# Attention: phi from transposed queries, its norms from narrow matmuls

## The chip, the cores and the metric
The program runs on one core of a Trainium2 chip. A core has five engines that run side by side and wait for each other on semaphores: PE (TensorE, matmuls and transposes), DVE (VectorE), ACT (ScalarE), POOL (GpSimd) and SP, which only issues DMAs here. The metric is the device time of one execution in microseconds (us).

## The reference
The program is one attention with a linear memory, then two mixture-of-experts layers. The change touches only the attention:

```
B, H, S, D = 4, 8, 576, 64
scores = (1/sqrt(D)) q k^T, causal;  a = softmax(scores);  local = a v
phi(x) = where(x > 0, x, exp(x) - 1) + 1          # = min(exp(x), 1) + max(x, 0)
q_p = phi(q)
mem_ret  = q_p M_prev            # (S x 64) (64 x 64) per batch and head
mem_norm = q_p . z_prev + 1e-6   # one number per row
g = sigmoid(beta)                # one number per head
out = g * mem_ret / mem_norm + (1 - g) * local
```

## The kernel before
The attention works through 16 units; unit u is one batch and one pair of heads. Each unit has 576 rows: four blocks of 128 and a tail of 64. The loop over u is software-pipelined in five slots n = 0 to 4: in slot n it issues the scores of a row block of unit u (`score`, blocks 3, 2, 1, 0 and the tail, which is block 4), a part of the second half of unit u-1, and a part of the transposes of unit u+1. A scheduler then places the instructions of each engine in one fixed order, in which they wait for semaphores; so the order is not quite that of the code.

The second half of a unit transposes the softmax numerators P (`ptrans`), and `av` accumulates both terms of the output in one PSUM tile x: first the memory term, `Mb` (M_prev of both heads on the diagonal) against `pT` (phi transposed), then P^T against v. The two heads of a pair each use 64 columns of the PE array, and their matmuls stand next to each other (L306). The result is multiplied with R (1 over the softmax sums, spread over 64 rows for each head, L307) into xT. So the memory term must hold g / mem_norm times the softmax sum before.

phi is made from the queries as they lie in memory (rows on the partitions, `phi_a`): exp on ACT (L126), max on POOL (L127), min and add on DVE (L128), times z on POOL (L131); DVE sums over d and inverts (`phi_b`, L149 to L153); POOL multiplies phi with the factor (L155, L167, `phi_c`). Then PE transposes the scaled phi (`trans` part 2) and ACT copies it to pT (L209). The sums' inverses go a way of their own: POOL spreads them to `rr` (L164), PE transposes them (L173, `inverse`), ACT copies them to R (L174). The tail's P is multiplied with its inverse sum on POOL (L255, `norm`).

PSUM tiles of the tag "t" (all transposes, x) have four buffers, so each waits for the copy out of the tile four before it. After units 3, 7, 11 and 15 the router of the first expert layer works on a batch of rows. The expert layers start when the attention and the router's table are done.

Of the kernel before, what the change touches and what calls it, by code (L numbers as in the profile page):

```python
# [19 lines left out]
NP = H // 2  # L20
# [7 lines left out]
def attention(ctx, tc, q, k, v, M_prev, z_prev, beta, xT, ident, router=None):  # L28
# [50 lines left out]
    Mb = []  # L79
    for i in range(2):  # L80
        t = c1.tile([128, NP, 128], F32, name=f"Mb{i}")
        nc.gpsimd.memset(t, 0.0)
        Mb.append(t)

    zt, ld, ph, un = {}, {}, {}, {}

    nrm, Rs = [], []
    for i in range(2):
        t = c1.tile([128, NT, 2], F32, name=f"nrm{i}")
        nc.vector.memset(t, 1.0)  # L90
        nrm.append(t)
        t = c1.tile([128, S], F32, name=f"R{i}")
        nc.gpsimd.memset(t[:, 512:], 1.0)
        Rs.append(t)

    def load_b(b):
        zt[b] = nat.tile([128, DM], F32, tag="z", name="zb", bufs=2)
        nc.sync.dma_start(zt[b], z_prev[b].rearrange("h d -> (h d)")[None, :].to_broadcast([128, DM]))
        for h in range(2):
            src = M_prev[b].rearrange("(a two) d e -> two d a e", two=2)[h]  # L100
            nc.sync.dma_start(Mb[b % 2][h * 64:(h + 1) * 64, :, h * 64:(h + 1) * 64], src)

    def load(u, names):

# [13 lines left out]

    def phi_a(u):

        b, a = divmod(u, NP)
        ex = tmp.tile([128, NT, 128], F32, tag="ex", name="ex")
        qp = tmp.tile([128, NT, 128], F32, tag="qp", name="qp")
        z = zt[b][:, a * 128:(a + 1) * 128]
        for e, p, qn in zip(parts(ex), parts(qp), parts(ld[u, "q"])):
            nc.scalar.activation(e, qn, AF.Exp)  # L126
            (nc.gpsimd if u else nc.vector).tensor_scalar(p, qn, 0.0, None, ALU.max)  # L127
            nc.vector.scalar_tensor_tensor(p, e, 1.0, p, ALU.min, ALU.add)  # L128
        zb = z[:, None, :].to_broadcast([128, 4, 128]), z[:64]
        for e, p, zz in zip(parts(ex), parts(qp), zb):  # L130
            nc.gpsimd.tensor_tensor(e, p, zz, ALU.mult)  # L131
        ph[u] = ex, qp
# [11 lines left out]
    def phi_b(u):  # L144

        a = u % NP
        ex, qp = ph[u]
        n = nrm[u % 2]
        nc.vector.tensor_reduce(n[:, :4], ex[:, :4].rearrange("p i (h d) -> p i h d", h=2), AX.X, ALU.add)  # L149
        nc.vector.tensor_reduce(n[:64, 4], ex[:64, 4].rearrange("p (h d) -> p h d", h=2), AX.X, ALU.add)  # L150
        nc.vector.tensor_scalar(n, n, 1e-6, None, ALU.add)
        nc.vector.reciprocal(n, n)
        nc.vector.tensor_tensor(n, n, gt[:, None, 2 * a:2 * a + 2].to_broadcast([128, NT, 2]), ALU.mult)  # L153
        pv = qp[:64, 4].rearrange("p (h d) -> p h d", h=2)
        nc.gpsimd.tensor_tensor(pv, pv, n[:64, 4, :, None].to_broadcast([64, 2, D]), ALU.mult)  # L155

    def phi_c(u):

        su, n = un[u]["su"], nrm[u % 2]
        nc.vector.tensor_scalar(su[:, :4], su[:, :4], 1e-9, None, ALU.add)  # L160
        rc = sm.tile([128, 4, 2], F32, tag="rc", name="rc", bufs=2)
        nc.vector.reciprocal(rc, su[:, :4])
        rr = un[u]["rr"] = tmp.tile([128, 4, 128], F32, tag="rr", name="rr")
        nc.gpsimd.tensor_copy(rr.rearrange("p i (h d) -> p i h d", h=2), rc[:, :, :, None].to_broadcast([128, 4, 2, D]))  # L164
        nc.vector.tensor_tensor(n[:, :4], n[:, :4], su[:, :4], ALU.mult)
        pv = ph[u][1][:, :4].rearrange("p i (h d) -> p i h d", h=2)
        nc.gpsimd.tensor_tensor(pv, pv, n[:, :4, :, None].to_broadcast([128, 4, 2, D]), ALU.mult)  # L167
# [8 lines left out]
    def phi_t(u):  # L176
        if "pT" not in un[u]:
            un[u]["pT"] = tr.tile([128, S], F32, tag="pT", name="pT")
        return un[u]["pT"]

    def trans(u, part):


        qt = qTp[u % 2]
        p = ps_t.tile([128, 512], F32, tag="t", name="tp")
        if part == 0:
            un[u] = {"kT": tr.tile([128, S], F32, tag="kT", name="kT"), "P": {}}
        if part < 3:
            src = (ld.get((u, "k")), ld.get((u, "q")), ph[u][1] if u in ph else None)[part]
            for i in range(4):  # L190
                nc.tensor.transpose(p[:, i * 128:(i + 1) * 128], src[:, i], ident)
        else:
            src = []
            if part == 3:
                src += [ld[u, "k"], ld[u, "q"]]
                if u > 0:
                    src.append(ph[u - 1][1])
            else:
                src += [ph[u][1]]
            for n, t in enumerate(src):  # L200
                nc.tensor.transpose(p[:, n * 64:(n + 1) * 64], t[:64, 4], ident[:64, :64])

        if part == 0:
            nc.vector.tensor_copy(un[u]["kT"][:, :512], p)
        elif part == 1:
            nc.scalar.activation(qt[:, 256:512], p[:, 256:], AF.Copy, scale=0.125)
            nc.vector.tensor_scalar(qt[:, :256], p[:, :256], 0.125, None, ALU.mult)
        elif part == 2:
            nc.scalar.copy(phi_t(u)[:, :512], p)  # L209
        elif part == 3:  # L210
# [3 lines left out]
            if u > 0:  # L214
                nc.vector.tensor_copy(phi_t(u - 1)[:, 512:], p[:, 128:192])
        else:
            nc.vector.tensor_copy(phi_t(u)[:, 512:], p[:, 0:64])

    def score(u, i):

# [3 lines left out]
        s = ps_s.tile([128, 2, 512], F32, tag="s", name="s")  # L224
        nm = sm.tile([128, 2], F32, tag="nm", name="nm")
        if i == 3:
            un[u]["su"] = sm.tile([128, NT, 2], F32, tag="su", name="su", bufs=2)
        sums = un[u]["su"][:, i]
        if i < 4:
            w = (i + 1) * 128  # L230
            for h in range(2):
# [18 lines left out]
    def norm(u):  # L250

        P, r = un[u]["P"][4], un[u]["su"][:, 4, 0:1]
        nc.vector.tensor_scalar(r, r, 1e-9, None, ALU.add)
        nc.vector.reciprocal(r, r)
        nc.gpsimd.tensor_scalar(P, P, r, None, ALU.mult)  # L255
# [64 lines left out]
    for u in range(NU + 1):  # L320
# [9 lines left out]
        for n in range(5):  # L330
            if sc:
                score(u, (3, 2, 1, 0, 4)[n])
                if n == 4:
                    phi_c(u)
            if ex:
                if n == 0:
                    norm(u - 1)
                    ptrans(u - 1, 5)
                    ptrans(u - 1, 4)
                elif n < 3:  # L340
                    ptrans(u - 1, 2 * n - 2)
                    ptrans(u - 1, 2 * n - 1)
                    if n == 1:
                        inverse(u - 1)
                    else:
# [942 lines left out]
```

## Time and profile before
| | before |
|---|---|
| median of 3 runs (lowest to highest) | 2078.16 us (2076.13 to 2081.61) |
| the profiled execution: its time, its span | 2078.23 us, 2076.5 us |
| busy share of the span: PE, DVE, ACT, POOL | 98%, 71%, 41%, 37% |
| scores of unit 3 start, scores of unit 15 start | 57.01 us, 252.83 us |
| last matmul of the attention ends about | 275.2 us |

The span is the time from the first to the last instruction that the profiler saw; the device time of that execution is 1.7 us longer. The attention is the first eighth of the span. A matmul in f32 shows as two records (two pieces, each with its own weight load, PEld); "x4" in a row is four such records one after the other. Ends of matmuls are modelled, so rates are read from starts.

### The profile page before, as it was taken

The page shows a single profiled execution, that of the slowest core. Times are in us where ns is not written, and L with a number is a line of the kernel's source. Part 1 is how long each engine was busy: PE and PEld are TensorE (multiplying, and loading weights), DVE is VectorE, ACT ScalarE, POOL GpSimd, SP SyncE. Part 2 cuts the span into 40 slices and gives each one's busy share as a digit, 9 for nine tenths or more (in the row PEclk, how much of TensorE's full clock was granted, in tenths as well). Part 3 has the DMA queues.
Part 4 walks back from the last instruction along what each step waited for, and adds up shares of the span by engine and source line. Part 5 has one row for each costly group of instructions (what it writes and reads, how often), then busy time and mean ns, then how long its engine had stood idle before and what let it go on. Part 6 is the DMA issues. An engine that isn't in the chain of part 4 may idle for free.

```text
span 2076.5 us, 31532 instructions
## 1 busy us (share of the span) xinstructions
PE 2038.2 (98%) x11528; PEld 1768.1 (85%) x11528; DVE 1480.6 (71%) x2573; ACT 853.7 (41%) x1808; POOL 776.9 (37%) x800
## 2 busy tenths in 40 slices
PE   7999999999899999999999999999999999999998
PEld 4666669999698998998888999899888899899987
DVE  6788757666786776667786677777678676677775
ACT  4656536555634333333343333333334433333332
POOL 6666511000133344344454334334355333333332
PEclk9999999999999999999999999999999999999999
DMA  7332146665611233444432222222223222122221
GB/s 189 83 75 78 33 153 229 202 210 170 215 51 61 68 67 69 62 66 77 61 107 67 61 77 66 62 76 67 62 62 111 62 63 80 61 64 79 62 62 40
DMA packets 238520, 187.35 MB, mean 90 GB/s; under 512 B 71440, under 2 KB 194320, under 8 KB 238352
## 3 DMA queue, kind: packets, MB, share of 16 engines
q1 hardware_dynamic: 229008, 171.48, 30.2%
q0 software_dynamic: 3520, 9.46, 1.3%
q10 hardware_dynamic: 5824, 4.25, 0.7%
q8 instruction: 95, 1.56, 0.3%
q14 instruction: 73, 0.60, 0.1%
HBM read 171.51 MB, written 13.64 MB: 89 GB/s over the span
## 4 chain that ended last, share of the span: by engine, by line
PE 46%; issue 16%; POOL 8%; DVE 3%; ACT 1%; POOLq 0%; DVEq 0%; ACTq 0%
PE y L1092 24%; PE prod L1021 21%; POOL T L913 4%; POOL w1l L907 3%; DVE w2l L907 0%; DVE c L1035 0%; DVE u L1035 0%; POOL out_dram L394 0%; DVE hl L1044 0%; PE lq L1133 0%; DVE S2l L907 0%; ACT hh L1039 0%; DVE A11l L907 0%; DVE A12l L907 0%; DVE csum L1166 0%
## 5 line engine op out<-in xcount | busy, mean ns | idle before, releaser
L1039 ACT ACTIVATE hh<-c 128x384 fp32r<-128x384 f32 x384 | 202.0, 526 | 837.3 <-DVE c L1035 837.2
L907 POOL TENSOR_TENSOR w1l<-T,w1h 128x1024 fp32r<-128x1024 f32 x94 | 226.7, 2412 | 851.0 <-ACT w1h L907 851.0
L1092 PE MATMUL y<-w2h,hh 128*128 128x512 f32 x1152 | 453.8, 394 | 0.0
L1092 PE MATMUL y<-w2l,hh 128*128 128x512 f32 x1152 | 453.8, 394 | 0.0
L1092 PE MATMUL y<-w2h,hl 128*128 128x512 f32 x1152 | 453.0, 393 | 0.0
L1044 DVE SCALAR_TENSOR_TENSOR hl<-c,hh 128x384 fp32r<-128x384 f32 x384 | 415.4, 1099 | 1.4 <-ACT hh L1039 1.0
L1035 DVE TENSOR_TENSOR c<-prod,u 128x384 f32<-128x384 f32 x288 | 160.3, 557 | 157.2 <-PE prod L1021 156.7
L1092 PEld LDWEIGHTS y<-w2h,hh 128*128 128x128 f32 x1152 | 216.5, 188 | 32.7
L1092 PEld LDWEIGHTS y<-w2h,hl 128*128 128x128 f32 x1152 | 216.5, 188 | 28.3
L1092 PEld LDWEIGHTS y<-w2l,hh 128*128 128x128 f32 x1152 | 216.7, 188 | 27.8
L913 POOL TENSOR_TENSOR T<-r,T 128x256 f32<-128x256 f32 x188 | 157.8, 840 | 14.1 <-issue 7.0
L913 POOL TENSOR_TENSOR T<-r 128x256 f32<-128x256 f32 x188 | 158.8, 845 | 7.1
L1035 DVE TENSOR_TENSOR u<-prod,u 128x384 f32<-128x384 f32 x192 | 106.0, 552 | 58.3 <-PE prod L1021 58.0
L1035 DVE TENSOR_TENSOR u<-prod,p 128x384 f32<-128x384 f32 x96 | 53.5, 557 | 127.2 <-PE prod L1021 127.1
L907 DVE TENSOR_TENSOR w2l<-r,w2h 128x512 fp32r<-128x512 f32 x188 | 137.1, 729 | 0.5 <-ACT w2h L907 0.5
L907 ACT CAST w2h<-r 128x512 fp32r<-128x512 f32 x188 | 106.7, 610 | 0.0
L907 DVE TENSOR_TENSOR w1l<-r,w1h 128x512 fp32r<-128x512 f32 (+1 forms) x188 | 104.6, 557 | 0.0
L1035 DVE TENSOR_TENSOR c<-prod,p 128x384 f32<-128x384 f32 x96 | 53.4, 557 | 68.8 <-PE prod L1021 64.1
L907 ACT CAST w1h<-T 128x1024 fp32r<-128x1024 f32 x94 | 97.0, 1032 | 1.0 <-POOL T L913 1.0
L1049 ACT COPY p<-prod 128x384 f32<-128x384 f32 x96 | 46.1, 480 | 120.8 <-PE prod L1021 120.6
L1103 DVE SCALAR_TENSOR_TENSOR acc<-y,P,acc 128x512 f32<-128x512 f32 x126 | 92.5, 744 | 4.3 <-PE y L1092 4.3
L907 ACT CAST w1h<-r 128x512 fp32r<-128x512 f32 (+1 forms) x188 | 94.5, 503 | 0.0
(386 smaller groups left out, 4202.9 us busy)
## 6 DMA issues: line engine op xcount, KB each, us to landing
r<-in_moe_w_dram SPq DMA_DIRECT2D x188, 512.0 KB, 4.5
r<-in_moe_w_dram SPq DMA_DIRECT2D x188, 256.0 KB, 2.9
xr<-xs_sorted SPq DMA_DIRECT2D x22, 256.0 KB, 5.1
kn<-in_k_dram SPq DMA_DIRECT2D x32, 128.0 KB, 2.6
qn<-in_q_dram SPq DMA_DIRECT2D x32, 128.0 KB, 2.7
vn<-in_v_dram SPq DMA_DIRECT2D x32, 128.0 KB, 2.8
xs_sorted<-zrow ACTq DMA_DIRECT2D x16, 256.0 KB, 3.1
zb<-in_z_prev_dram SPq DMA_DIRECT2D x4, 256.0 KB, 3.8
```

What stands on the lines that cost most here:

```text
L907: return (lambda: nc.scalar.copy(hi, src)), (lambda: eng.tensor_tensor(lo, src, hi.bitcast(F32), ALU.subtract))
L913: sub = lambda i, a, b: (lambda: nc.gpsimd.tensor_tensor(T[:, i], a, b, ALU.subtract))
L1021: nc.tensor.matmul(p, a[:, kd], b[:, kd], start=(i == 0), stop=(i == 5))
L1035: nc.vector.tensor_tensor(st[o], a, st[b], ALU.add)
L1039: nc.scalar.activation(hh[:, f, a * HT:(a + 1) * HT], st[o], AF.Relu)
L1044: nc.vector.scalar_tensor_tensor(hl[:, f, w], st[o], 0.0, hh[:, f, w].bitcast(F32), ALU.max, ALU.subtract)
L1049: nc.scalar.copy(st["p1"], p)
L1092: nc.tensor.matmul(yt[t], a[:, f, t * 128:(t + 1) * 128], b[:, f], start=(j == 0 and f == 0 and i == 0), stop=(j == NJ - 1 and f == 1 and ...
L1103: nc.vector.scalar_tensor_tensor(acc[t], yt[t], P[:, m, e:e + 1], acc[t], ALU.mult, ALU.add)
```

## The change
phi is now made from the transposed queries, which the scores need anyway (`qTp`, scaled by 1/8, so exp and relu take scale 8): exp and relu on ACT, min and add on DVE, straight into pT. The norms come from five matmuls for each unit whose stationary operand is a 128-column block of pT and whose moving operand is `Zb`, 128 x 2: z of one head in each column (tile `nb`). `sums` inverts norms and softmax sums together, multiplies the first four blocks' norm inverses with the sums, spreads all to `rr` (now 9 x 128 wide) and scales the tail's P. `inverse` transposes two sets of four blocks instead of one: the first multiplies pT in place on DVE, the second goes to R. The tail's block of `rr` is transposed in `ptrans` k = 7. g is multiplied into Mb when it is loaded; z is loaded as a column instead of spread over 128 partitions.

```diff
     def load_b(b):
-        zt[b] = nat.tile([128, DM], F32, tag="z", name="zb", bufs=2)
-        nc.sync.dma_start(zt[b], z_prev[b].rearrange("h d -> (h d)")[None, :].to_broadcast([128, DM]))
+        z = nat.tile([128, NP], F32, tag="z", name="zc", bufs=2)
+        zv = z_prev[b].rearrange("(a two) d -> two d a", two=2)
         for h in range(2):
+            r = slice(h * 64, (h + 1) * 64)
+            nc.sync.dma_start(z[r], zv[h])
...
+            nc.gpsimd.tensor_tensor(Mb[b % 2][r, :, r], Mb[b % 2][r, :, r],
+                                    gtm[r, :, None].to_broadcast([64, NP, D]), ALU.mult)
+            nc.gpsimd.tensor_copy(Zb[b % 2][r, :, h], z[r])
     def phi_a(u):
...
+        nc.scalar.activation(ex[:, :512], qt[:, :512], AF.Exp, scale=8.0)
+        nc.scalar.activation(rl[:, :512], qt[:, :512], AF.Relu, scale=8.0)
+        p = un[u]["pT"] = tr.tile([128, S], F32, tag="pT", name="pT")
+        nc.vector.scalar_tensor_tensor(p, ex, 1.0, rl, ALU.min, ALU.add)
+    def phi_b(u):
...
+        x = ps_t.tile([128, NT, 2], F32, tag="t", name="nb")
+        for i in range(NT):
+            o = min(i * 128, S - 128)
+            nc.tensor.matmul(x[:, i], un[u]["pT"][:, o:o + 128], Zb[b % 2][:, a], start=True, stop=True)
+        nc.vector.tensor_scalar(un[u]["nw"][:, :NT], x, 1e-6, None, ALU.add)
+    def sums(u):
...
+        nc.vector.tensor_scalar(nw[:, n:w], nw[:, n:w], 1e-9, None, ALU.add)
+        nc.vector.reciprocal(iv[:, :w], nw[:, :w])
+        nc.vector.tensor_tensor(iv[:, :8], iv[:, :8], nw[:, n:n + 8], ALU.mult)
+        rr = un[u]["rr"] = tmp.tile([128, 9, 128], F32, tag="rr", name="rr")
+        nc.gpsimd.tensor_copy(rr.rearrange("p i (h d) -> p (i h) d", h=2), iv[:, :18, None].to_broadcast([128, 18, D]))
+        P = un[u]["P"][4]
+        nc.gpsimd.tensor_scalar(P, P, iv[:, w - 1:w], None, ALU.mult)
     def inverse(u):
-        p = ps_t.tile([128, 512], F32, tag="t", name="rp_")
-        for i in range(4):
-            nc.tensor.transpose(p[:, i * 128:(i + 1) * 128], un[u]["rr"][:, i], ident)
-        nc.scalar.copy(Rs[u % 2][:, :512], p)
+        pT = un[u]["pT"]
+        for n in range(2):
+            p = ps_t.tile([128, 512], F32, tag="t", name="rp_")
+            for i in range(4):
+                nc.tensor.transpose(p[:, i * 128:(i + 1) * 128], un[u]["rr"][:, 5 * n + i], ident)
+            if n == 0:
+                nc.vector.tensor_tensor(pT[:, :512], pT[:, :512], p, ALU.mult)
+            else:
+                nc.scalar.copy(Rs[u % 2][:, :512], p)
     def ptrans(u, k):
...
+            nc.tensor.transpose(p[:, 128:256], un[u]["rr"][:, 4], ident)
+            pT = un[u]["pT"]
+            nc.vector.tensor_tensor(pT[:, 512:], pT[:, 512:], p[:, 192:256], ALU.mult)
...
             if ex:
                 if n == 0:
-                    norm(u - 1)
+                    sums(u - 1)
...
                     if n == 1:
                         inverse(u - 1)
-                    else:
-                        trans(u - 1, 2)
```

On PE, early in a steady unit, between the transposes of P blocks 2 and 3 and the next scores, before the change (tp is the PSUM tile of a transpose, kn the keys):

```order
L276 MATMUL tp_1440<-ident,P_1273 128x128
L276 MATMUL tp_1440<-ident,P_1235 128x128
L276 MATMUL tp_1440<-ident,P_1273 128x128
L276 MATMUL tp_1440<-ident,P_1235 128x128
L191 MATMUL tp<-ident,kn 128x128 x4
L233 MATMUL s<-kT,qTp_134 128x384 x2
```

and after:

```order
L258 MATMUL tp_1607<-ident,P_1450 128x128
L258 MATMUL tp_1607<-ident,P_1407 128x128
L258 MATMUL tp_1607<-ident,P_1450 128x128
L258 MATMUL tp_1607<-ident,P_1407 128x128
L142 MATMUL nb<-Zb_147,pT 128x2 x5
L190 MATMUL tp<-ident,kn 128x128 x4
L222 MATMUL s<-kT,qTp_139 128x384 x2
```

The five norm matmuls stand in front of the key transposes, and all later work of PE in the unit stands behind them.

On PE, later in the unit, from the transposes of the tail's P to the tail's scores, before the change:

```order
L283 MATMUL tp_1532<-ident,P_1381 128x128 x4
L289 MATMUL tp_1539<-ident,P_1381 64x128
L298 MATMUL x<-pT,Mb_140 128x256
L306 MATMUL x<-pt,vn 64x256 x2
L306 MATMUL x<-pt,vn 64x128 x2
L201 MATMUL tp<-ident,kn 128x64
L201 MATMUL tp<-ident,qn 128x64
L201 MATMUL tp<-ident,qp 128x64
L243 MATMUL s<-kT,qTp_134 128x288 x2
```

and after:

```order
L265 MATMUL tp_1517<-ident,P_1363 128x128 x4
L271 MATMUL tp_1524<-ident,P_1363 64x128
L283 MATMUL x<-pT,Mb_145 128x256
L291 MATMUL x<-pt,vn 64x256
L273 MATMUL tp_1524<-ident,rr 128x128
L291 MATMUL x<-pt,vn 64x256
L291 MATMUL x<-pt,vn 64x128 x2
L193 MATMUL tp<-ident,kn 128x64
L193 MATMUL tp<-ident,qn 128x64
L232 MATMUL s<-kT,qTp_139 128x288 x2
```

The tail's transpose of `rr` (L273) now stands between the matmuls of the two heads (the pair 64x256). It stands so in 13 of the 16 units; in the other three it splits the pair 64x128.

On POOL, one steady unit, from one scaling of the tail's P to the next, before:

```order
L255 TENSOR_SCALAR P_927<-P_927,su 128x576
L141 TENSOR_TENSOR vn<-vn,om 128x512
L142 TENSOR_TENSOR vn<-vn,om 64x128
L127 TENSOR_SCALAR qp<-qn 128x512
L127 TENSOR_SCALAR qp<-qn 64x128
L131 TENSOR_TENSOR ex<-qp,zb 128x512
L131 TENSOR_TENSOR ex<-qp,zb 64x128
L164 COPY rr<-rc 128x512
L167 TENSOR_TENSOR qp<-qp,nrm_142 128x512
L155 TENSOR_TENSOR qp<-qp,nrm_146 64x128
L255 TENSOR_SCALAR P_1115<-P_1115,su 128x576
```

and after:

```order
L152 TENSOR_TENSOR vn<-vn,om 128x512
L153 TENSOR_TENSOR vn<-vn,om 64x128
L167 TENSOR_SCALAR P_1738<-P_1738,iv 128x576
L165 COPY rr<-iv 128x1152
L152 TENSOR_TENSOR vn<-vn,om 128x512
L153 TENSOR_TENSOR vn<-vn,om 64x128
L167 TENSOR_SCALAR P_1921<-P_1921,iv 128x576
```

Five of POOL's instructions are gone, and the spread of the inverses, which stood ahead of the scaling of the tail's P, now stands behind it.

## Rows read from the trace of the kernel before

**Rows 1.** Windows: stretch, us, busy us of PE, PEld, DVE, ACT, POOL; clock, DMA, GB/s.
```profile
25.00:30.00 5.00, 2.89 (x12) 1.81 (x13) 4.74 (x16) 2.99 (x8) 2.90 (x4) 0.68 0.89 219
57.01:252.83 195.82, 192.14 (x1380) 120.97 (x1377) 154.14 (x409) 116.30 (x350) 117.84 (x133) 1.00 0.27 69
106.94:121.91 14.97, 14.53 (x110) 9.24 (x106) 12.69 (x32) 9.81 (x31) 9.58 (x12) 1.00 0.24 54
121.91:136.26 14.35, 14.33 (x109) 9.26 (x105) 11.89 (x30) 9.00 (x29) 8.69 (x11) 1.00 0.36 83
```

**Rows 2.** Waits of PE's weight loads, 57.01 to 252.83: us, times, longest.
```profile
PEld x L298 <- ACT pT L209: 3.8, 12, 0.4
...
PEld tp L191 <- issue: 1.6, 3, 0.6
...
PEld x L298 <- DVE pt L290: 1.5, 3, 0.6
```

**Rows 3.** Timeline of the expert stage at the f32 matmul with 8 columns.
```profile
588.73 0.28 PE L1025 MATMUL prod<-csum,one 128*128 128x8 f32 x2
588.84 0.19 PEld L1092 LDWEIGHTS y<-w2l,hh 128*128 128x128 f32 x1
588.86 0.48 PE L1092 MATMUL y<-w2l,hh 128*128 128x512 f32 x1
588.95 0.19 PEld L1092 LDWEIGHTS y<-w2h,hl 128*128 128x128 f32 x1
```

**Rows 4.** Timeline of PE in the unit that starts at 121.91.
```profile
126.13 0.60 PE L173 MATMUL rp__1669<-ident,rr 128*128 128x128 f32 x4
126.57 0.60 PE L191 MATMUL tp<-ident,qn 128*128 128x128 f32 x4
...
130.04 0.27 PE L289 MATMUL tp<-ident,P 128*64 128x128 f32 x1
130.34 0.70 PE L298 MATMUL x<-pT,Mb 128*128 128x256 f32 x2
130.97 0.87 PE L306 MATMUL x<-pt,vn 128*64 128x256 f32 x8
131.77 0.27 PE L201 MATMUL tp<-ident,kn 64*128 64x64 f32 x1
...
133.19 0.78 PE L298 MATMUL x<-pT,Mb 128*128 128x320 f32 x2
```

**Rows 5.** Timeline of PE: a head pair split by router transposes, and one whole.
```profile
88.29 1.12 PE L233 MATMUL s<-kT,qTp 64*128 64x512 f32 x2
89.34 0.66 PE L507 MATMUL lp<-ident,lt 128*128 128x128 f32 x4
...
106.94 1.13 PE L233 MATMUL s<-kT,qTp 64*128 64x512 f32 x4
108.00 0.29 PE L235 MATMUL s<-mk,idb 128*128 128x128 bf16 x2
```

**Rows 6.** Groups by line, 57.01 to 252.83: busy us, mean ns, idle before.
```profile
L255 POOL TENSOR_SCALAR P<-P,su 128x576 f32<-128x576 f32 x12 | 20.7, 1723 | 1.0 <-DVE nrm L150 1.0
...
L128 DVE SCALAR_TENSOR_TENSOR qp<-ex,qp 128x512 f32<-128x512 f32 (+1 forms) x24 | 17.7, 736 | 18.1 <-POOL qp L127 18.1
...
L164 POOL COPY rr<-rc 128x512 f32<-128x512 f32 x12 | 7.3, 609 | 23.1 <-DVE nrm L165 23.1
```

**Rows 7.** Timeline of the last unit: tail scores, their exp, P's scaling, inverses.
```profile
263.61 0.19 PE L244 MATMUL s<-mk,idb 128*128 128x64 bf16 x1
...
265.26 0.19 ACT L247 ACTIVATION_READ_ACCUMULATOR P<-s,nm 128x1 f32 x1
...
266.02 1.73 POOL L255 TENSOR_SCALAR P<-P,su 128x576 f32<-128x576 f32 x1 [2.34 <-DVE su L254]
...
268.29 0.38 PE L173 MATMUL rp__3447<-ident,rr 128*128 128x128 f32 x2
```

**Rows 8.** Timeline of PE in the second unit, at the second block of scores.
```profile
27.11 1.65 PE L233 MATMUL s<-kT,qTp 64*128 64x384 f32 x4 [2.80 <-ACT P L247]
```

More of the change, by code (lines that the diff above doesn't have):

```diff
@@ L71, in attention @@
     nc.vector.tensor_scalar(om, gt, -1.0, 1.0, ALU.mult, ALU.add)
+    gtm = c1.tile([128, NP], F32, name="gtm")
+    gtv = gt.rearrange("p (a two) -> p a two", two=2)
+    nc.vector.tensor_copy(gtm[0:64], gtv[0:64, :, 0])
+    nc.vector.tensor_copy(gtm[64:128], gtv[64:128, :, 1])
     qTp = []
@@ L78, in attention @@
         qTp.append(t)
-    Mb = []
+    Mb, Zb = [], []
     for i in range(2):
[L81 to L87, printed above, removed]
+        for to, nm, w in ((Mb, "Mb", 128), (Zb, "Zb", 2)):
+            t = c1.tile([128, NP, w], F32, name=f"{nm}{i}")
+            nc.gpsimd.memset(t, 0.0)
+            to.append(t)
+    ld, ph, un = {}, {}, {}
+    Rs = []
     for i in range(2):
-        t = c1.tile([128, NT, 2], F32, name=f"nrm{i}")
-        nc.vector.memset(t, 1.0)
-        nrm.append(t)
         t = c1.tile([128, S], F32, name=f"R{i}")
@@ L96, in load_b @@
     def load_b(b):
-        zt[b] = nat.tile([128, DM], F32, tag="z", name="zb", bufs=2)
-        nc.sync.dma_start(zt[b], z_prev[b].rearrange("h d -> (h d)")[None, :].to_broadcast([128, DM]))
+        z = nat.tile([128, NP], F32, tag="z", name="zc", bufs=2)
+        zv = z_prev[b].rearrange("(a two) d -> two d a", two=2)
         for h in range(2):
+            r = slice(h * 64, (h + 1) * 64)
+            nc.sync.dma_start(z[r], zv[h])
             src = M_prev[b].rearrange("(a two) d e -> two d a e", two=2)[h]
-            nc.sync.dma_start(Mb[b % 2][h * 64:(h + 1) * 64, :, h * 64:(h + 1) * 64], src)
+            nc.sync.dma_start(Mb[b % 2][r, :, r], src)
+            nc.gpsimd.tensor_tensor(Mb[b % 2][r, :, r], Mb[b % 2][r, :, r],
+                                    gtm[r, :, None].to_broadcast([64, NP, D]), ALU.mult)
+            nc.gpsimd.tensor_copy(Zb[b % 2][r, :, h], z[r])
     def load(u, names):
@@ L119, in phi_a @@
     def phi_a(u):
-        b, a = divmod(u, NP)
[L122 to L132, printed above, removed]
+        ex, rl = ph[u]
+        qt = qTp[u % 2]
+        nc.scalar.activation(ex[:, :512], qt[:, :512], AF.Exp, scale=8.0)
[3 more added lines that the diff above has]
+    def phi_b(u):
+        b, a = divmod(u, NP)
+        x = ps_t.tile([128, NT, 2], F32, tag="t", name="nb")
[3 more added lines that the diff above has]
+        nc.vector.tensor_scalar(un[u]["nw"][:, :NT], x, 1e-6, None, ALU.add)
     def gate_v(u):
@@ L142, in gate_v @@
         nc.gpsimd.tensor_tensor(l, l, g[:64, :, None].to_broadcast([64, 2, D]), ALU.mult)
[L144 to L167, printed above, removed]
@@ L169, in inverse @@
-    def inverse(u):
-        p = ps_t.tile([128, 512], F32, tag="t", name="rp_")
-        for i in range(4):
-            nc.tensor.transpose(p[:, i * 128:(i + 1) * 128], un[u]["rr"][:, i], ident)
-        nc.scalar.copy(Rs[u % 2][:, :512], p)
[L176 to L179, printed above, removed]
+    def sums(u):
+        nw = un[u]["nw"].rearrange("p i h -> p (i h)")
+        iv = sm.tile([128, 4 * NT], F32, tag="iv", name="iv", bufs=2)
+        n, w = 2 * NT, 4 * NT - 1
+        nc.vector.tensor_scalar(nw[:, n:w], nw[:, n:w], 1e-9, None, ALU.add)
[5 more added lines that the diff above has]
+        nc.gpsimd.tensor_scalar(P, P, iv[:, w - 1:w], None, ALU.mult)
@@ L187, in trans @@
             un[u] = {"kT": tr.tile([128, S], F32, tag="kT", name="kT"), "P": {}}
-        if part < 3:
-            src = (ld.get((u, "k")), ld.get((u, "q")), ph[u][1] if u in ph else None)[part]
+        if part < 2:
+            src = ld[u, "kq"[part]]
             for i in range(4):
@@ L192, in trans @@
         else:
[L193 to L197, printed above, removed]
-            else:
-                src += [ph[u][1]]
-            for n, t in enumerate(src):
-                nc.tensor.transpose(p[:, n * 64:(n + 1) * 64], t[:64, 4], ident[:64, :64])
+            for n, nm in enumerate("kq"):
+                nc.tensor.transpose(p[:, n * 64:(n + 1) * 64], ld[u, nm][:64, 4], ident[:64, :64])
         if part == 0:
@@ L207, in trans @@
             nc.vector.tensor_scalar(qt[:, :256], p[:, :256], 0.125, None, ALU.mult)
-        elif part == 2:
-            nc.scalar.copy(phi_t(u)[:, :512], p)
-        elif part == 3:
+        else:
             nc.vector.tensor_copy(un[u]["kT"][:, 512:], p[:, 0:64])
@@ L213, in trans @@
             nc.vector.tensor_scalar(qt[64:128, 576:640], p[64:128, 64:128], 0.125, None, ALU.mult)
[L214 to L217, printed above, removed]
+            ph[u] = [tmp.tile([128, S], F32, tag=t, name=t) for t in ("ex", "rl")]
+            nc.scalar.activation(ph[u][0][:, 512:], p[:, 64:128], AF.Exp)
+            nc.vector.tensor_scalar(ph[u][1][:, 512:], p[:, 64:128], 0.0, None, ALU.max)
     def score(u, i):
@@ L226, in score @@
         if i == 3:
-            un[u]["su"] = sm.tile([128, NT, 2], F32, tag="su", name="su", bufs=2)
-        sums = un[u]["su"][:, i]
+            un[u]["nw"] = sm.tile([128, 2 * NT, 2], F32, tag="nw", name="nw", bufs=2)
+        sums = un[u]["nw"][:, NT + i]
         if i < 4:
@@ L248, in score @@
         un[u]["P"][i] = P
[L250 to L255, printed above, removed]
     def ptrans(u, k):
@@ L359, in attention @@
                     gate_v(u)
-                elif n == 3 and u + 1 == NU:
-                    trans(u, 4)
             if u + 1 < NU:
```

3 lines of the change are left out of this document (removed).

## The prediction
> **What bounds the kernel now.** I read the windows first. Over twelve units, from the fourth unit's first scores at 57.01 to the sixteenth's at 252.83, PE is busy 192.14 of 195.82 us, DVE 154.14, ACT 116.30, POOL 117.84 [rows 1]. A busy PE is not yet PE at its peak, so I then read where its weight loads waited for another engine in that stretch. The waits that this change can touch are 3.8 us for the copy of phi (pT), 1.5 for the tail's P, and 1.6 at transposes that waited for a free PSUM tile [rows 2]; the others belong to the router, which stays. Last I read one unit in order of time: that from 121.91 to 136.26 takes 14.35 us, of which PE is busy 14.33 at full clock, and the unit before it 14.97 with 14.53 [rows 1]. So in the steady attention PE sets the pace with its own work, and there is little waiting to give back. POOL and DVE wait for each other (DVE 18.1 us for POOL's max [rows 6]), but these waits end before PE needs the result. What follows the attention waits for its end, so a microsecond there is a microsecond of the kernel.
>
> **The change part by part.** Each unit's PE work, then what waits.
>
> *Norm matmuls.* Five f32 matmuls are ten pieces, each with a 128x128 weight load and only 2 moving columns. The nearest row is the expert stage's f32 matmul with 8 columns: its two pieces start at 588.73 and PE's next matmul at 588.86; the weight loads behind it follow at 588.84 and 588.95, 0.11 apart [rows 3]. Four f32 transposes, also one weight load each, take 126.13 to 126.57, 0.11 each [rows 4]. I take 0.11 a piece, 1.10 a unit. Ends: nothing, if the loads hide under other matmuls, and 0.19, what the load record lasts [rows 3], 1.90 a unit.
>
> The Trainium skill (TensorE: Matmul & The Clock Gate, Back-to-back issue gap) gives about 25 ns as the floor from start to start for up to 64 columns, and says itself that this isolated gap holds no weight load. By that floor alone the ten pieces would be an estimated 0.25 us a unit and the sum below 7 instead of 18. The 0.11 between loads in the rows speaks for the load as the price.
>
> *Transposes.* The second set of inverses adds four, 0.44; the scaled phi's four go, so these cancel. Phi's 64-row tail transpose goes too, which I leave at nothing.
>
> *The split pair.* The tail's inverse transpose stands between the two heads of a 256-column pair in 13 units. Two heads next to each other share the array: both pieces of both heads of 512 columns take 106.94 to 108.00, 1.06; one head alone, split off by router transposes, takes 88.29 to 89.34, 1.05 [rows 5]. So a split pair pays for the second head in full. The eight pieces of the 256- and 128-column pairs take 130.97 to 131.77, 0.80 [rows 4]; three fifths to two thirds of it, about 0.48 or a little more, belong to the 256 pair. I add 0.48 and 0.11 for the transpose itself: 0.59. Ends: 0.11 (the neighbours fill the gap) and 0.8.
>
> So PE gets 1.10 + 0.59 = 1.69 us a unit, 20.3 in the twelve units (one of them splits the 128 pair only, 0.24 less).
>
> *What PE gets back.* pT no longer comes from a late ACT copy: it is scaled by DVE right after the inverses are transposed, well ahead of the memory matmul. That wait shows as 130.04 to 130.34, 0.30, where a piece takes 0.11 anyway [rows 4], so of the 3.8 about 2.4 come back; of the other 1.5 and 1.6, with three pieces each, 1.2 and 1.3. Together 4.9. Twelve units: 20.3 - 0.2 - 4.9 = +15.2.
>
> *POOL, DVE, ACT.* POOL loses the max, both products with z and with the factor, and grows the spread from 512 to 1152 columns: 609 ns [rows 6] x 1152/512 = 1.37. DVE loses two reductions and 18.1 us of waiting, and gains a product over 128x512 and a wider min-and-add; in the unit of 14.35 us it is busy 11.89 and ACT 9.00 [rows 1]. I cost both at nothing: 2.5 us of idle DVE time cover the rest. If the additional PSUM tile of a unit makes a transpose wait as in rows 2, it is up to 0.6 a unit (longest there), and that is the upper end.
>
> *The inverses' way.* The spread now stands behind the scaling of the tail's P on POOL, and PE's transposes wait for it. In the last unit the tail's scores end at 263.61, the accumulated sum starts at 265.26, the scaling starts at 266.02 and PE is at the inverses at 268.29 [rows 7]. New: 266.02 + 1.72 + 1.37 = 269.1, with one more short DVE instruction ahead 269.3: PE waits 1.0 there. In a steady unit the spread is done about 5.7 after the tail's scores; PE gets there after 136.26 - 133.19 of output matmuls [rows 4], 126.13 - 121.91 of the next unit [rows 1, 4] and the 1.10 of norm matmuls: 8.4. The order costs nothing there, by 2.7 us; without that cover it would be 1 us a unit.
>
> *Start and end.* In the second unit PE waits 2.80 for the exp of the tail [rows 8], late because DVE waits for POOL, and the stretch from 25 to 30 runs at a mean clock of 0.68 with PE busy 2.89 [rows 1]; with DVE free of POOL up to 2.8 + 1.4 = 4.2 come back. Against it stand 1.69 in each of the first three units, 5.1, and an inverse chain as long as in the last unit. I take 0 for the three, ends -4.2 and +5.1. The sixteenth unit's scores: +1.69 less one wait of 0.2, +1.5. The last unit's second half: 0.59 + 1.0 - 0.2, +1.4.
>
> *DMAs.* For each of four batches one load of 256 KB becomes two of 1 KB in 4-byte pieces, on SP and ahead of v and the next k. POOL waits for them, then multiplies Mb; with five instructions less it has the time, and Zb is first read after phi. Nothing, in the steady units.
>
> Sum: 15.2 + 1.5 + 1.4 + 0 = 18.1. The profiled execution took 2078.23 (its span 2076.5 and 1.7 around it), 0.07 above the median of 2078.16. 2078.2 + 18 = **2096**.
>
> **Rivals.** *Hidden loads (not slower).* If the norm matmuls' weight loads run under the long score matmuls around them, the 1.10 goes to nothing: 13 units x 1.10 = 14.3 off, and with the start's 4.2 the time is 2078. For it: the load of the first of two pieces at 588.73 is not seen as a gap [rows 3]. Against: ten stand in a row with nothing long between them, and the next loads keep 0.11. It decides once the ten take under 0.4 us together (18.1 - 13 x 0.7 - 4.2 = 4.8, inside what counts as no change).
>
> The Trainium skill (TensorE: Matmul & The Clock Gate, Step-by-step: what each phase is for) says that PE pulls weight loads ahead of running matmuls where they go to the background weight buffer. By that rule the first of the ten hides; the trace shows no case of ten.
>
> *Dear loads.* Each piece takes 0.19: 13 x 0.8 = 10.4 more, 2107. For it only the record's length; against it that the next load starts after 0.11 [rows 3].
>
> *Relief (faster).* DVE's 18.1 us of waits for POOL vanish, and that shows as time. PE's idle time in the twelve units is 195.82 - 192.14 = 3.7 us [rows 1], which is all that could come back there, with 4.2 at the start; it outweighs the added work only if nearly all of the 1.69 is hidden. Time: 2078 - 8 = 2070.
>
> *A small loss.* The pair refills itself (0.11 for 0.59) and the start gives its 4.2: 18.1 - 13 x 0.48 - 4.2 = 7.7, or 2086, with somewhat cheaper pieces 2083.
>
> **Numbers.** Forecast, slower by 9 to 30 us: 0.72. Dear loads 0.09, of which the range holds half. A small loss 0.09, half of it under 0.3%. Hidden loads 0.06. Faster 0.04. Runs of before span 2076.13 to 2081.61, so about 0.3%, 6 us, is what a measurement tells from no change. From the cases: slower 0.72 + 0.09 + 0.045 = 0.855, same 0.105, faster 0.04. The range from 2086 to 2109 leaves out hidden loads, relief, the small loss and the top of the dear loads, about 0.2.
>
> **What would show it.** Right: steady units of 15.5 to 16 us with PE still busy to within 0.3; ten pieces at L142 0.11 apart; the memory matmul (L283) without a wait; about 0.5 more between L283 and the key tails; a wait at the inverses in the last unit only; the attention ending near 293. Wrong: norm pieces closer than 0.05, or steady units at 14.4 with the pieces inside former gaps; waits of nb or of the inverses on DVE or POOL in each unit, which would make it slower than said; a clock below 1.0 in the steady units; or a second unit shorter by more than 4 us.

## The result and the profile after

| | before | after |
|---|---|---|
| median (lowest to highest), four runs each | 2079.18 us (2076.13 to 2081.61) | 2101.38 us (2098.85 to 2106.48) |
| the profiled execution: its time, its span | 2078.23 us, 2076.5 us | 2100.08 us, 2098.4 us |
| scores of unit 3 start, scores of unit 15 start | 57.01, 252.83 us | 59.51, 271.46 us |
| last output matmul of the attention starts | 275.02 us | 295.95 us |

The change makes the kernel slower: the ratio is 1.0111, with a 95% interval of 1.0086 to 1.0135. Of the 21.9 us by which the span grew, 2.5 lie ahead of the fourth unit, 16.1 in the twelve units (195.82 to 211.95), 2.3 from the sixteenth unit's scores to the last output matmul, and 0.9 behind the attention, where nothing was changed.

Windows of the kernel after, as in [rows 1]: the first unit, the twelve units, one steady unit.

```profile
10.52:25.49 14.97, 12.76 (x55) 7.63 (x55) 6.83 (x15) 7.86 (x26) 8.86 (x46) 0.68 0.84 221
59.51:271.46 211.95, 210.68 (x1500) 138.22 (x1497) 139.85 (x345) 118.79 (x352) 66.57 (x70) 1.00 0.24 61
114.15:130.05 15.90, 15.90 (x119) 10.58 (x115) 10.68 (x24) 9.23 (x28) 4.21 (x5) 1.00 0.25 57
```

In the twelve units PE is busy 18.5 us longer and idle 2.4 us less; POOL fell from 117.84 to 66.57 and DVE from 154.14 to 139.85, and neither shows in the time of a steady unit. The twelve lengths fall into four kinds: the units that took 14.35 now take 15.91 (three, +1.55 each); those that took 14.97 to 15.03 now also take 15.91 (three, +0.9 each, since they lost a wait); the three that end with the router's logits grew by 0.63 each, since the logits' wait for xT got shorter; the three behind a router batch by 2.54, 1.30 and 3.00.

The waits of PE's weight loads from 59.51 to 271.46 that answer to [rows 2]: those for pT, for the tail's P and at a free PSUM tile are gone, and one is new, eleven times 0.4 for the copy that reads the PSUM tile into which L273 writes. It lies under the matmul ahead of L273: PE itself is not idle there. The logits' wait for xT (L466), which the prediction left to the router, is 1.5 where it was 4.3 (the last line, from the kernel before).

```profile
PEld tp L273 <- DVE pt L272: 4.2, 11, 0.4
PEld lq L466 <- DVE xT L292: 1.5, 3, 0.5
```

```profile
PEld lq L487 <- DVE xT L307: 4.3, 3, 1.4
```

The timeline of PE in the unit from 114.15 (answers to [rows 4]):

```profile
115.99 1.18 PE L142 MATMUL nb<-Zb,pT 128*128 128x2 f32 x10
117.03 0.64 PE L190 MATMUL tp<-ident,kn 128*128 128x128 f32 x4
...
119.45 0.60 PE L175 MATMUL rp__1466<-ident,rr 128*128 128x128 f32 x4
119.88 0.60 PE L175 MATMUL rp__1472<-ident,rr 128*128 128x128 f32 x4
...
123.35 0.27 PE L271 MATMUL tp<-ident,P 128*64 128x128 f32 x1
123.46 0.60 PE L283 MATMUL x<-pT,Mb 128*128 128x256 f32 x2
123.99 0.65 PE L291 MATMUL x<-pt,vn 128*64 128x256 f32 x2
124.56 0.33 PE L273 MATMUL tp<-ident,rr 128*128 128x128 f32 x1
124.82 0.86 PE L291 MATMUL x<-pt,vn 128*64 128x256 f32 x6
125.62 0.27 PE L193 MATMUL tp<-ident,kn 64*128 64x64 f32 x1
```

The ten norm pieces take 115.99 to 117.03, 0.104 each. The memory matmul L283 follows L271 after 0.11, without a wait. One head of the 256-column pair alone takes 0.57, the transpose between the heads 0.26, the other six pieces 0.80: 1.63 from 123.99 to 125.62, where the eight pieces took 0.80 before [rows 4].

In two of the three units behind a router batch (from 92.96 and 234.21) the scheduler put the norm pieces ahead of the 384-column scores and the four key transposes between their two heads, which stood next to each other before the change (PE, from 99.06):

```profile
99.06 1.28 PE L142 MATMUL nb<-Zb,pT 128*128 128x2 f32 x10
100.27 0.91 PE L222 MATMUL s<-kT,qTp 64*128 64x384 f32 x2
101.11 0.66 PE L190 MATMUL tp<-ident,kn 128*128 128x128 f32 x4
101.70 0.91 PE L222 MATMUL s<-kT,qTp 64*128 64x384 f32 x2
102.54 0.28 PE L224 MATMUL s<-mk,idb 128*128 128x128 bf16 x2
```

Each head takes 0.84 there; in the run without the norm matmuls (below) both together take 0.85. In the third of these units (from 163.73) other matmuls stand between the two heads, but so they did in the kernel before:

```profile
157.94 0.91 PE L233 MATMUL s<-kT,qTp 64*128 64x384 f32 x2
...
160.90 0.91 PE L233 MATMUL s<-kT,qTp 64*128 64x384 f32 x2
```

In the last unit (answers to [rows 7]) the spread ends at 288.55, and PE waits 0.69 for it:

```profile
285.74 1.72 POOL L167 TENSOR_SCALAR P<-P,iv 128x576 f32<-128x576 f32 x1 [11.89 <-DVE iv L162]
287.41 1.14 POOL L165 COPY rr<-iv 128x1152 f32<-128x1152 f32 x1
...
288.61 0.66 PE L175 MATMUL rp__3387<-ident,rr 128*128 128x128 f32 x4 [0.69 <-POOL rr L165]
```

At the start, two rows of ACT (ACTq is its sequencer, which issues DMAs) and one of PE. ACT's first exp could have started at about 14.1, when DVE's maxima were done (a reduction of 1.21 from 12.87). It starts at 15.42, behind three DMAs that clear the router's rows. Then PE waits 1.83, and the granted clock from 16.90 to 25.30 is 0.50 (1.2 GHz), with PE busy 8.38 of 8.40. In the kernel before DVE's maxima come at 16.34, and the two DMAs that ACT issues ahead of its exp end at 15.73. In the profiled executions both kernels spend 10.2 us at half clock ahead of the fourth unit: before the change from 9.74 to 16.57 and from 26.81 to 30.22, after it from 15.87 to 26.11.

```profile
13.96 1.41 ACTq L455 DMA_DIRECT2D xs_sorted<-zrow  x3
15.42 0.69 ACT L228 ACTIVATE P<-s,nm 128x512 f32<-128x512 f32 x1 [3.29 <-POOL gap L372]
```

```profile
16.92 1.22 PE L222 MATMUL s<-kT,qTp 64*128 64x256 f32 x2 [1.83 <-ACT P L228]
```

### The profile page after: what moved, and what is told of

It reads as the page before. It is cut to its first block, busy times and chain, and to the rows that moved or that the text cites. A ratio compares the mean times of both kernels' runs of the same rounds, so it can differ in the third digit from the quotient of the medians.

```text
span 2098.4 us, 31656 instructions
## 1 busy us (share of the span) xinstructions
PE 2064.5 (98%) x11686; PEld 1791.3 (85%) x11688; DVE 1460.1 (70%) x2491; ACT 856.4 (41%) x1808; POOL 711.5 (34%) x724
## 4 chain that ended last, share of the span: by engine, by line
PE 45%; issue 16%; POOL 8%; DVE 3%; ACT 1%; POOLq 0%; DVEq 0%; ACTq 0%
PE y L1071 24%; PE prod L1000 21%; POOL T L892 4%; POOL w1l L886 3%; DVE w2l L886 0%; DVE c L1014 0%; DVE u L1014 0%; POOL out_dram L373 0%; DVE hl L1023 0%; PE lq L1112 0%; DVE S2l L886 0%; ACT hh L1018 0%; DVE A11l L886 0%; DVE A12l L886 0%; DVE csum L1145 0%
```

## The experiments

All start from the changed kernel, but for one. "Steady unit" is a unit away from the router, "fourth" the start of the fourth unit's scores; these and the twelve units are read from one profiled execution each.

| run | median us | ratio to before, 95% | steady unit | fourth | twelve units |
|---|---|---|---|---|---|
| before | 2079 to 2081 | 1 | 14.35 to 15.03 | 57.01 | 195.82 |
| changed | 2101.4 | 1.0111, 1.0086 to 1.0135 | 15.91 | 59.51 | 211.95 |
| without norm matmuls | 2089.0 | 1.0039, 1.0025 to 1.0053 | 14.83 | 61.20 | 200.97 |
| tail's rr first | 2094.0 | 1.0058, 1.0041 to 1.0075 | 15.18 | 59.63 | 206.22 |
| norms in bf16 | 2093.9 | 1.0065, 1.0048 to 1.0082 | 15.00 | 61.87 | 202.85 |
| clearing DMAs on POOL | 2099.3 | 1.0089, 1.0072 to 1.0106 | 15.91 | 55.17 | 213.42 |
| three edits | 2080.0 | 0.9995, 0.9986 to 1.0005 | 14.27 | 58.42 | 193.95 |
| three edits, two bf16 parts | 2083.0 | 1.0010, 1.0000 to 1.0019 | 14.53 | 55.99 | 196.21 |
| before, clearing on POOL | 2082.1 | 1.0007, 0.9998 to 1.0017 | 14.35 to 14.92 | 57.57 | 197.90 |
| norms late | 2108.5 | 1.0132, 1.0116 to 1.0148 | 16.04 | 66.23 | 214.09 |
| all, bf16 | 2076.5 | 0.9978, 0.9968 to 0.9988 | 14.32 | 57.69 | 192.85 |
| all, two bf16 parts | 2086.6 | 1.0026, 1.0017 to 1.0035 | 14.57 | 59.54 | 196.50 |
| tail's P scaled on ACT, one run | 2106.3 | | 15.91 | 64.19 | 212.90 |
| changed, again, one run | 2101.5 | | 15.91 | 60.64 | 213.34 |

**Without the norm matmuls.**

```diff
...
-            nc.tensor.matmul(x[:, i], un[u]["pT"][:, o:o + 128], Zb[b % 2][:, a], start=True, stop=True)
-        nc.vector.tensor_scalar(un[u]["nw"][:, :NT], x, 1e-6, None, ALU.add)
+        nc.vector.memset(un[u]["nw"][:, :NT], 64.0)
```

> The changed kernel without the five norm matmuls of a unit; the norms are set to a constant, so the output lacks them. Theory (each piece's weight load is a price on PE): 1.04 us a unit comes back, 12.5 in the twelve units, and in the units after a router batch, where the ten pieces stand between the two heads of the 384-column scores, another 0.84, 2.5 for the three. The twelve units go from 211.95 to about 197, a steady unit from 15.91 to 14.87, the time from 2101 to 2081 or 2085. Rival (the loads are hidden and the time went elsewhere): 2098 to 2101, steady units stay at 15.9.

Measured: a steady unit fell by 1.08, as the theory said; the pieces are on PE's path, and the rival of hidden loads falls. The time fell by 12.4, to 4 above the higher of the two times expected: the start took 1.7 longer, and the units behind a batch did not give what was expected. There four transposes, not the ten norm pieces, stand between the heads of the changed kernel, and newly so in two units, not three. In these two the pair is whole again, but they got shorter by 1.2 and 1.0 instead of 1.9; the third took 21.94 instead of 21.12. In all three PE now waited for the copy ahead of the tail's rr (0.57, 1.08 and 1.08), where PE itself does not wait in the changed kernel. The whole 384-column pair, on PE:

```profile
99.43 0.92 PE L218 MATMUL s<-kT,qTp 64*128 64x384 f32 x4
100.28 0.28 PE L220 MATMUL s<-mk,idb 128*128 128x128 bf16 x2
```

**The tail's rr first.**

```diff
-            nc.vector.tensor_copy(un[u]["pt4"], p[:64, 0:128].rearrange("p (h q) -> p h q", h=2))
             nc.tensor.transpose(p[:, 128:256], un[u]["rr"][:, 4], ident)
+            nc.vector.tensor_copy(un[u]["pt4"], p[:64, 0:128].rearrange("p (h q) -> p h q", h=2))
```

> The tail's rr is transposed before the copy out of the same PSUM tile, so that it stands ahead of the memory matmul and no longer between the two heads of a 256-column pair; nothing is left out. Theory (the split pair and the wait for the copy are the price): the stretch from the first head to the key tails goes from 1.63 to about 0.80 and the transpose's own 0.11 stays, so a steady unit goes from 15.91 to 15.2, the twelve units from 212 to about 203.5, the time to about 2090. Rival (the transpose itself and its wait are the price, the pair refills the array): at most 0.3 a unit, 2097 to 2101.

Measured: 15.18, and the pair is whole again. So the broken pair costs 0.73 a unit, and the transpose alone 0.11. The edit also takes away L273's wait for the copy; the timeline of the changed kernel tells the two apart. The head ahead of L273 takes 0.57, and two f32 pieces of as many columns in L283, with no wait behind them, take 0.53; so by an estimate the wait holds 0.04 of the 0.73. The time fell by 7.4, to 4 above what was expected. The profiled execution was the slowest of four (2096.69, the others 2090.75 to 2096.09); in it PE ran at half clock from 238.06 to 241.47, 4.5 us behind a wait of 0.27 for the router, which stands in the changed kernel without such a fall.

```profile
121.41 0.27 PE L272 MATMUL tp<-ident,rr 128*128 128x128 f32 x1
121.52 0.60 PE L283 MATMUL x<-pT,Mb 128*128 128x256 f32 x2
122.05 0.87 PE L291 MATMUL x<-pt,vn 128*64 128x256 f32 x8
122.85 0.27 PE L193 MATMUL tp<-ident,kn 64*128 64x64 f32 x1
```

**Norms in bf16.**

```diff
...
+        ph[u] = tr.tile([128, S], BF16, tag="pB", name="pB")
+        nc.gpsimd.tensor_copy(ph[u], p)
...
-            nc.tensor.matmul(x[:, i], un[u]["pT"][:, o:o + 128], Zb[b % 2][:, a], start=True, stop=True)
+            nc.tensor.matmul(x[:, i], ph[u][:, o:o + 128], Zb[b % 2][:, a], start=True, stop=True)
```

> The norm matmuls in bf16: POOL makes a bf16 copy of pT, z is rounded to bf16, five pieces instead of ten; the norms lose their low bits. Theory (the f32 weight load of 128 columns is the price, and the router's narrow bf16 matmuls stand 0.03 apart): the five take about 0.15 instead of 1.04, a steady unit 15.0, the time about 2087. Rival (each narrow matmul costs 0.10 whatever its type): 0.52 instead of 1.04, steady unit 15.4, time about 2093.

Measured: the five take 115.53 to 115.66, 0.026 each, a quarter of an f32 piece, and a steady unit 15.00, as the theory said. So a narrow matmul is cheap in bf16 and dear in f32, and the rival falls. That the f32 weight load is the dear part fits the f32 transposes, which move 128 columns and also stand 0.11 apart; but load and matmul changed their type together, so no run parts them. The time fell by half of what was expected: the fourth unit starts 2.4 later, behind a wait of 4.57 for POOL's copy of pT in the first unit, and the pairs behind a batch stay broken.

```profile
115.53 0.27 PE L144 MATMUL nb<-Zb,pB 128*128 128x2 bf16 x5
115.66 0.63 PE L192 MATMUL tp<-ident,kn 128*128 128x128 f32 x4
```

```profile
17.87 0.30 PE L144 MATMUL nb<-Zb,pB 128*128 128x2 bf16 x5 [4.57 <-POOL pB L136]
```

The Trainium skill (TensorE: Matmul & The Clock Gate, Weight-path perf modes) says that weights load faster where there are 128 of them and their type is not FP32. The two figures, 0.104 and 0.026, agree with that. The floor of about 25 ns that the prediction cited from the Trainium skill (TensorE: Matmul & The Clock Gate, Back-to-back issue gap) is what the bf16 matmuls show, weight loads included; the f32 pieces stay four times above it.

**The clearing DMAs on POOL's queue.**

```diff
-                nc.scalar.dma_start(self.xs[e * N + r * 128:e * N + (r + 1) * 128], z)
+                nc.gpsimd.dma_start(self.xs[e * N + r * 128:e * N + (r + 1) * 128], z)
```

> The DMAs that clear the sorted rows are issued by POOL's queue instead of ACT's; nothing is left out. Theory (in the first unit ACT, whose maxima are ready at 14.0, issues three of these DMAs until 15.4 before its first exp, PE then waits 1.8 us and falls to half clock from about 16 to 26): ACT's first exp starts near 14.1, the fourth unit's scores start at 56 to 58 instead of 59.5, the time falls by 1 to 3. Rival (the start lost its time to the norm matmuls and to the loads of z): the fourth unit still starts at 59 to 60.

Measured: ACT's first exp at 14.43, PE does not wait for it, the first unit 11.49 instead of 14.97, the fourth unit at 55.17, 4.3 earlier and earlier than the theory said. A part of this can be the clock: the half clock lasts 6.8 us here (11.86 to 18.69), 10.2 in the changed kernel. The time fell by 2.0, within its scatter; the unit from 159.39, behind a batch, took 22.55 instead of 21.12, and the stretch behind the attention was longer.

**The tail's P scaled on ACT.**

```diff
-        nc.gpsimd.tensor_scalar(P, P, iv[:, w - 1:w], None, ALU.mult)
+        nc.scalar.activation(P, P, AF.Copy, scale=iv[:, w - 1:w])
```

> The changed kernel with the tail's P scaled on ACT instead of POOL, so that the spread of the inverses no longer stands behind that scaling; nothing is left out. Theory (the 1.73 of the scaling ahead of the spread is what PE waits for): the waits at the first set of inverses in the second unit (1.4) and in the last (0.7) vanish, steady units keep 15.9 since the spread is in time there. Rival (the inverses are late because the reciprocal is late): both waits stay at 0.5 or more.

Measured (one run, 2106.27): both waits are gone, and the stretch from the sixteenth unit's scores to the last output matmul fell from 24.49 to 23.58. So the scaling ahead of the spread was what PE waited for. The run was slower all the same: in the third unit an exp of ACT stood behind the last two clearing DMAs, which take 0.34 each but start 2.90 apart, and PE waited 2.55 and fell to half clock. What ACT's queue waited for between them is not shown. In the changed kernel the last one starts 4.01 behind the one ahead of it (43.12 and 47.13), and PE waits only 0.73 there.

```profile
45.61 0.34 ACTq L455 DMA_DIRECT2D xs_sorted<-zrow  x1
...
48.51 0.34 ACTq L455 DMA_DIRECT2D xs_sorted<-zrow  x1
```

```profile
50.39 0.70 PE L222 MATMUL s<-kT,qTp 64*128 64x256 f32 x2 [2.55 <-ACT P L228]
```

**Three edits together**: the tail's rr first, norms in bf16 (the copy by DVE in the first two units), clearing on POOL.

> Three edits together: the tail's rr transposed ahead of the copy, norms from five bf16 matmuls (the bf16 copy of pT by DVE in the first two units, by POOL after them), the clearing DMAs on POOL's queue; the norms lose their low bits. Theory (the three prices are PE's own and add): steady units 15.91 - 0.73 - 0.91 = 14.27, the fourth unit's scores start at 52 to 54, the twelve units take 192 to 194, the time is 2071 to 2076, below the kernel before. Rival (what PE gets back is taken by the next wait, as the medians of the single edits, 7.4, 7.5 and 2, seem to say): 2083 to 2086.

Measured: steady units and the twelve as the theory said, 14.27 and 193.95, so the prices add; the time, 2080.0, lies between the two, at that of the kernel before. The start missed: 58.42. There ACT had to issue the load of the gate weights, which waits for a memset on POOL, now behind the clearing DMAs and a wait of 1.76 for v; its exps and copies stood behind it, and PE waited 3.83.

```profile
34.26 0.41 ACTq L393 DMA_DIRECT2D wg<-in_moe_w_gate_dram  x1
34.72 0.47 ACT L230 ACTIVATE P<-s,nm 128x256 f32<-128x256 f32 x1 [5.01 <-POOL gap L374]
```

```profile
36.16 0.69 PE L293 MATMUL x<-pt,vn 128*64 128x128 f32 x4 [3.83 <-ACT pt L254]
```

**Two bf16 parts.** As in the run with three edits, but pT and z are each a sum of two bf16 parts and the norm a sum of three products:

```diff
...
+        nc.vector.tensor_tensor(ph[u][1], p, ph[u][0], ALU.subtract)
...
+            for n, (c, w) in enumerate(((0, 0), (0, 2), (1, 0))):
+                nc.tensor.matmul(x[:, i], ph[u][c][:, o:o + 128], Zb[b % 2][:, a, w:w + 2], start=(n == 0), stop=(n == 2))
```

> As the run with three edits, but pT and z are each split into two bf16 parts, and the norm is the sum of three products of parts: fifteen bf16 matmuls a unit instead of ten f32 pieces; the second part of pT is made by DVE. Theory (each narrow bf16 matmul 0.027): 0.40 instead of 1.04, steady units 14.55, twelve units 196 to 197, time 2075 to 2081, the kernel before within 0.3%. Rival (DVE's additional product or PE's wait for it takes the gain): steady units 15 or more, time 2083 to 2090.

Measured: 14.53 and 196.21, as the theory said; the time, 2083.0, missed by 2, at the edge of the rival's range. Its steady units rule that rival out. From the last output matmul to the end its profiled execution took 1808.1, 5.7 more than that of the changed kernel; the cause of this stays open.

**The kernel before with the clearing on POOL.**

> The kernel before with the clearing DMAs on POOL's queue. Theory (in the kernel before DVE, not ACT's queue, delays the first exp): the fourth unit's scores stay at 56.5 to 57.5 and the time at 2079 to 2081. Rival (the DMAs cost the kernel before as much as the changed one): the fourth unit starts at 53 to 55, the time is 2076 to 2078; or POOL, which has more to do there, is late and the time is above 2083.

Measured: 57.57 and 2082.1, a little above what the theory allowed. The DMAs' queue does not help the kernel before, which agrees with its first exp waiting for DVE.

**Norms late**: the five f32 norm matmuls three slots later.

```diff
-                if n == 0:
-                    phi_b(u)
-                elif n == 2:
+                if n == 2:
                     gate_v(u)
+                elif n == 3:
+                    phi_b(u)
```

> The changed kernel with its five f32 norm matmuls issued three slots later, behind the output matmuls of the first half; nothing is left out. Theory (in the three units after a router batch the ten pieces stand between the two heads of the 384-column scores, and that pair then costs 0.84 more): these units go from 21.2 to about 20.3, steady units stay at 15.9, the time falls by 2 to 3, to 2098 or 2099. Rival (those units are long because of the router's own waits): 21.2 as before, time 2101.

Measured: a miss. A steady unit rose by 0.13, and the start lost 6.7 us (the first unit ran at a clock of 0.50, the second at a mean of 0.87). In the two units whose pair the key transposes had broken, the pair is whole, and they fell by 0.6 and 0.4; the third, whose pair is broken in either order, took 23.02. PE again waited in all three ahead of the tail's rr (0.17, 1.08 and 0.66). So this run gives the price of the broken 384-column pair only roughly; it is read from the two timelines above (1.68 in two heads, 0.85 together).

**All edits**: the tail's rr first, bf16 norms three slots later, clearing and gate weights on POOL's queue; then the same with two bf16 parts.

> Tail's rr transposed ahead of the copy, bf16 norm matmuls issued three slots later, and both the clearing DMAs and the loads of the gate weights on POOL's queue, so that none of ACT's DMAs waits for a POOL instruction; the norms lose their low bits. Theory (steady units 14.27; the stall of the run with three edits, PE 3.8 us and then half clock, came from ACT's DMA of the gate weights waiting for POOL's memset): the fourth unit's scores start at 52 to 54, the twelve units take 190 to 192, the time is 2070 to 2074, faster than the kernel before by 0.3 to 0.5%. Rival (the start stalls at another place): fourth unit at 57 to 59, time 2076 to 2080, the same as before.

> The same with pT and z split into two bf16 parts each and fifteen matmuls a unit, so that the norms keep their bits. Theory: steady units 14.53, fourth unit's scores at 53 to 55, twelve units 193 to 195, time 2073 to 2078, 0.1 to 0.35% below the kernel before. Rival (DVE's additional product is in PE's way now that the norms come late, or the start stalls): 2080 to 2084.

Measured: the bf16 version takes 2076.5, faster than the kernel before by 0.2% (0.1 to 0.3%), at the price of the norms' low bits. Its steady units are 14.32 and the units behind a batch 19.0, 20.8 and 18.9. The run with three edits, with steady units of 14.27 and the pair broken in the first and last of these, has 19.8, 20.6 and 19.9: 0.7 and 1.0 more where the pair is broken, which agrees with 0.83. The start missed again (57.69): PE waited 0.70, 1.22 and 0.69 for exps and 1.03 for the spread, and the first unit ran at a mean clock of 0.51. The time is within the rival's range, and so is the start. The version with all bits has steady units of 14.57 but takes 2086.6, slower than before and outside both ranges; its fourth unit starts at 59.54, and its twelve units take 196.50.

```profile
10.50:23.71 13.21, 12.51 (x50) 7.21 (x51) 7.75 (x16) 7.95 (x26) 12.97 (x28) 0.51 0.87 250
57.69:250.54 192.85, 190.35 (x1440) 124.20 (x1436) 138.45 (x345) 117.56 (x352) 74.22 (x82) 1.00 0.26 67
```

**The changed kernel again.**

> The changed kernel once more, unaltered, for the start of another execution. Theory (PE's wait for ACT's first exp, behind the clearing DMAs, recurs and with it the half clock): the fourth unit's scores start within 1 us of 59.5, and steady units take 15.91 again. Rival (the clock falls at another place in each execution): the fourth unit starts more than 1 us away, and the starts of the other runs say nothing of their edits.

Measured: 2101.52; fourth unit at 60.64, 1.1 from 59.51, so neither theory holds as it was put: the half clock recurred, but PE did not wait for ACT's first exp. The steady units and the second and third unit agree to 0.01. The first unit took 15.81 instead of 14.97, this time at a clock of 0.50 throughout and with PE busy in all of it; one unit behind a batch took 22.44 instead of 21.12. So differences of about 1 us in the first unit, or in one unit behind a batch, mean nothing between single executions. The 4.3 of the clearing DMAs is more than that, but the half clock lasts 17.1 us here (9.65 to 26.71), 10.2 in the first execution and 6.8 in that run, so it is not told how much of the 4.3 is the DMAs'.

```profile
10.81:26.62 15.81, 15.81 (x56) 9.41 (x56) 6.84 (x15) 7.85 (x26) 9.11 (x48) 0.50 0.84 219
```

## Why the prediction was right, step by step

The forecast was 2096 with a range of 2086 to 2109, slower; 2101.4 was measured, and by the mechanism that was named. Hidden loads, Relief and A small loss fall with the run without norm matmuls and with that of the tail's rr: both prices are paid in full. Dear loads fall with 0.104 a piece. (The sum by the floor of 25 ns alone comes to 7.05, not to below 7.) The terms:

- *Norm matmuls*, 1.10 a unit: 1.04 in the timeline, 1.08 by leaving them out. Right.
- *The split pair*, 0.59 a unit: mis-sized; 0.83, of which 0.11 is the transpose. The 0.48 for the second head came as a share of a whole pair's 0.80. One head alone takes 0.57, and from the transpose to the next head 0.26 pass instead of 0.11. Why is open: the wait for the copy out of its PSUM tile does not explain it, since the same 0.26 stand in the second unit, where L273 does not wait (37.82 to 38.08).
- *Twelve units*, +15.2: +16.1, so near in part by luck. The waits for pT and for the tail's P came back as said, and PE's idle time fell by 2.4. Errors both ways nearly cancel. The split pair costs 0.24 more than said in each unit, 2.9. In two of the three units behind a batch the key transposes break a second pair, 0.83 each, 1.7; the prediction read the new order in a steady unit only. Against that, the wait of the router's logits for xT, which was to stay, fell by 2.8, and the norm matmuls took 0.7 less.
- *First three units*, 0: +2.5 (3.6 in the second execution). This step failed. It set up to 4.2 of relief, from DVE, against 5.1 of added work and took them to cancel. DVE was indeed early, PE's first scores start 0.97 earlier, and the wait of 2.80 is gone. But other waits stand in its place: 1.83 for ACT's exp behind the clearing DMAs, 1.41 for the spread, 0.73 for ACT's copy of P. From the first to the fourth unit's scores PE's waits fell only from 5.7 to 4.6, and the half clock lasts 10.2 us in both profiled executions. How much the clearing DMAs cost is not settled. With them off ACT's queue the fourth unit starts 1.8 earlier than in the kernel before, in one execution. Across all versions of the changed kernel the first unit took 11.1 to 14.5 with those DMAs on POOL's queue (five runs, four of them with other edits too) and 14.8 to 17.3 with them on ACT's (seven). But in the second execution of the changed kernel PE did not wait for ACT's first exp at all, and the first unit was longer.
- *Sixteenth unit and last half*, +2.9: +2.3. PE's wait for the inverses is 0.7, said to be 1.0; the spread took 1.14 instead of 1.37. The same wait also stands in the second unit (1.41); the prediction names that chain for the start, but its signs have the wait in the last unit only.
- *POOL, DVE, ACT and the loads at nothing*, steady units: right; PE is busy in all of the 15.90. POOL has six instructions a unit less (ten before, four after), not five.

What stays open: why the half clock at the start lasts 6.8 us in one run and 17.1 in another, and why the stretch behind the attention took 1801.3 to 1808.1 us among the profiled executions, with the same code there. No run bears on either.

## What to carry to other kernels

Read the new order for every kind of unit, not only the steady one, and look for what lands between matmuls that share the array: one transpose of 0.11 us cost 0.73 more there, and moving one line undid it. An f32 matmul piece of 2 columns cost 0.10 us, as much as a transpose of 128; in bf16 it took a quarter. An engine that issues a DMA whose data another engine must prepare holds everything behind it in its queue (ACT 5.0 us and PE 3.8 in the run with three edits), so such issues belong on a queue with nothing urgent behind them.

## What was not expected of the hardware

In one execution of the changed kernel the first unit ran at a granted clock of 0.50 (1.2 GHz) from its first to its last matmul, 15.81 us in which PE was busy throughout, behind a wait of 2.24. In the other execution it began at full clock behind a wait of 2.05 and lost it behind one of 1.83. A clearing DMA took POOL's queue 0.54 us to issue (six in 3.25) and ACT's 0.34 to 0.52 in the changed kernel; but on ACT's queue the last two started 4.01 us apart there, and 2.90 in another run, with nothing issued between them.
